# Where a partition's rows lie in DRAM: two runs of 785 and 367 rows in place of a block per transfer

## The chip, the cores and the metric

One core of a Trainium2 chip runs the kernel; the seven others are idle. The metric is the device time of one execution in microseconds (us), the median of several.

A ratio of two kernels is the mean time of one kernel's runs over that of the other's in the same rounds, with a 95% interval. It is thus not quite the quotient of the medians that are quoted beside it.

## The reference

```python
H = W = 384; C = 384; k = 1          # x: 1 x 384 x 384 x 384 in bf16, w1d: one number
g = jnp.einsum("bhwc->bc", x) / (H * W)
s = jax.nn.sigmoid(g * w1d[0])       # with k = 1 the convolution is one product
return x * s[:, None, None, :]
```

The gate s needs the mean over all 147,456 rows, so no row can be scaled before all were read. A row is 384 bf16 numbers, 768 B; each of 128 partitions gets 1152 rows, 884,736 B. The kernel keeps 367 rows per partition on the chip (296 of them folded, four into the space of three), and 785 are streamed through for the sum and read a second time for the product.

## The kernel before: the parts that matter

```python
def view(t, r0, n):                  # n rows a partition, one block of 128 n rows in DRAM
    return t[r0 * P : (r0 + n) * P, :].rearrange("(p r) c -> p r c", r=n)
...
def load(chunk, a, lo=0, hi=None):   # rows lo to hi of each partition's piece of the chunk
    r0, n = chunk
    ...  nc.sync.dma_start(out=arena[:, a : a + hi - lo, :], in_=view(xf, r0, n)[:, lo:hi, :])
...
def stream(n, a):
    load((streamed[0], n), a)        # a chunk of its own for each transfer
    ...  sum_rows(a, n)              # one matmul a row, into one accumulator
```

A chunk (r0, n) is a block of 128 n consecutive rows in DRAM, and partition p's piece of it is n rows starting at row p n of the block. The distance from one partition's piece to the next, the pitch, is therefore n x 768 B and depends on the transfer: 36,864 B for 48 rows. All large transfers are issued on one queue. While the stores and the second loads run, VectorE multiplies by s in place and restores the folded rows.

## Time and profile before

| quantity | value | from |
|---|---|---|
| time | 722.86 us (721.91 to 723.49) | 3 runs |
| span of the profiled run | 721.1 us | page |
| VectorE busy | 69% | busy times |
| TensorE busy | 30% | busy times |
| 16 DMA engines busy | 98.7% | table of queues |
| read and written | 190.41 and 113.25 MB | table of queues |

The table is read by asking which resource has no room left. It is the DMA engines; the lines of the page and of the stretches that carry this stand in the prediction. The chain of waits changes hands often (DMA 52%, VectorE 29% of it), but where VectorE is in the chain, DMA engines are still busy with other transfers, except at the turn from reading to writing.

### The profile page before, as it was taken

To read this page: it belongs to the slowest core of one execution; us is meant where nothing else is said; L and a number is where in the kernel's file an instruction comes from. 1 tells how busy PE (TensorE), PEld (TensorE's weight loads), DVE (VectorE), ACT (ScalarE), POOL (GpSimd) and SP (SyncE) were. 2 spreads that over 40 slices of the span, in tenths; PEclk is the share of its full clock that TensorE was granted. 3 is DMA by queue.
4 is the path that set the end of the run, shared out by engine and by line. 5 is a ranking of instruction groups with operands and counts; after the bars stand their busy time and mean duration, and the time that the engine had idled before them with its cause. 6 is when DMAs were issued, how large, how long until landed. Compare 5 with 4: busy or idle time off the path is not lost.

```text
span 721.1 us, 3241 instructions
## 1 busy us (share of the span) xinstructions
PE 212.8 (30%) x1202; PEld 118.5 (16%) x1202; DVE 496.3 (69%) x469; ACT 115.4 (16%) x92; POOL 0.2 (0%) x4
## 2 busy tenths in 40 slices
PE   4687788988877770000000000000000000000000
PEld 2344444554544340000000000000000000000000
DVE  4600003987999819999999998999979994355330
ACT  3600002765777610001100000000000000000000
POOL 0000000000000000000000000000000000000000
PEclk9899999999999995555555555555555555555555
DMA  9999999999999978999999999999999999999997
GB/s 377 438 432 426 429 433 428 435 431 425 430 422 429 426 329 333 413 426 427 436 429 439 423 431 436 433 439 426 419 432 433 440 437 427 426 435 437 438 428 321
DMA packets 19602, 303.87 MB, mean 421 GB/s; under 512 B 2178, under 2 KB 2178, under 8 KB 6402
## 3 DMA queue, kind: packets, MB, share of 16 engines
q1 hardware_dynamic: 19584, 303.67, 98.7%
q8 instruction: 9, 0.15, 0.1%
q14 instruction: 7, 0.06, 0.0%
q10 hardware_dynamic: 2, 0.00, 0.0%
HBM read 190.41 MB, written 113.25 MB: 421 GB/s over the span
## 4 chain that ended last, share of the span: by engine, by line
DMA 52%; DVE 29%; PE 6%; another core or an unknown queue 4%; ACT 3%; SPq 0%; issue 0%; DVEq 0%
DMA arena<-in_x_dram 37%; DVE arena L434 18%; DMA out_dram<-arena 15%; DVE arena L251 7%; PE bank L227 6%; DVE arena L257 4%; ACT arena L291 3%; SPq L221 0%; ACT s_bf L425 0%; PE bank L506 0%; DVE odd L501 0%; DVE odd_i L510 0%; DVE worst L496 0%; DVEq L112 0%
## 5 line engine op out<-in xcount | busy, mean ns | idle before, releaser
L434 DVE TENSOR_TENSOR arena<-arena,s_bf 128x1536 bf16<-128x1536 bf16 (+8 forms) x102 | 241.9, 2413 | 73.7 <-DMA arena<-in_x_dram 56.9
L251 DVE TENSOR_SCALAR arena<-arena 128x1536 uint16<-128x1536 uint16 (+2 forms) x247 | 145.9, 635 | 109.2 <-DMA arena<-in_x_dram 97.6
L227 PE MATMUL bank<-arena,ones 128*128 128x384 bf16 x1152 | 204.6, 339 | 55.0 <-DMA arena<-in_x_dram 54.9
L227 PEld LDWEIGHTS bank<-arena,ones 128*128 128x128 bf16 x1152 | 113.6, 101 | 145.7 <-DMA arena<-in_x_dram 60.4
L257 DVE TENSOR_TENSOR arena<-arena 128x1536 uint16<-128x1536 uint16 (+2 forms) x114 | 121.2, 1063 | 10.4 <-PE bank L227 8.3
L291 ACT ACTIVATE arena<-arena 128x3072 uint16<-128x3072 uint16 (+1 forms) x38 | 102.5, 2696 | 142.9 <-DVE arena L251 142.9
L361 ACT COPY arena<-bank 128x512 uint32<-128x512 uint32 (+1 forms) x7 | 4.0, 570 | 70.3 <-DMA out_dram<-arena 70.1
L242 PE MATMUL bank<-ones,zeros 128*128 128x384 bf16 x48 | 8.3, 326 | 0.0
L291 ACT ACTIVATION_READ_ACCUMULATOR arena<-arena 128x1 f32 x38 | 7.1, 187 | 0.0
L242 PEld LDWEIGHTS bank<-ones,zeros 128*128 128x128 bf16 x48 | 4.7, 98 | 3.1
L506 PE MATMUL bank<-odd,ones 128*128 128x1 bf16 x1 | 0.2, 187 | 15.8 <-DVE odd L501 15.8
L361 ACT COPY bank<-arena 128x512 uint32<-128x512 uint32 (+1 forms) x7 | 3.6, 565 | 0.0
L425 ACT ACTIVATE s_bf<-bank,w_sc 128x384 bf16<-128x384 f32 x1 | 0.6, 580 | 15.3 <-PE bank L227 15.3
L506 PEld LDWEIGHTS bank<-odd,ones 128*128 128x128 bf16 x1 | 0.1, 105 | 16.2 <-DVE odd L501 16.2
L721 ACT ACT_TABLE_LOAD x1 | 1.3, 1283 | 0.7 <-PEq L737 0.7
L321 DVE TENSOR_SCALAR w_sc<-bank 128x1 f32<-128x1 f32 x1 | 0.2, 160 | 1.1 <-PE bank L316 1.1
L311 DVE MEMSET ones<- 128x128 bf16 x1 | 0.2, 165 | 1.0 <-SPq L106 1.0
L316 PE MATMUL bank<-w_bf,ones 1*128 1x1 bf16 x1 | 0.2, 182 | 2.1 <-DMA w_bf<-in_w1d_dram 2.1
L316 PEld LDWEIGHTS bank<-w_bf,ones 1*128 1x128 bf16 x1 | 0.1, 100 | 2.1 <-DMA w_bf<-in_w1d_dram 2.1
L510 DVE CAST odd_i<-bank 128x1 int32<-128x1 f32 x1 | 0.2, 159 | 0.3 <-PE bank L506 0.3
L496 DVE TENSOR_REDUCE worst<-seen 128x1 f32<-128x38 f32 x1 | 0.2, 189 | 0.0
L501 DVE TENSOR_SCALAR odd<-worst 128x1 bf16<-128x1 f32 x1 | 0.2, 156 | 0.0
(5 smaller groups left out, 0.5 us busy)
## 6 DMA issues: line engine op xcount, KB each, us to landing
arena<-in_x_dram SPq DMA_DIRECT2D x17, 4608.0 KB, 34.7
out_dram<-arena SPq DMA_DIRECT2D x6, 4608.0 KB, 43.8
arena<-in_x_dram SPq DMA_DIRECT2D x19, 1248.0 KB, 11.7
arena<-in_x_dram SPq DMA_DIRECT2D x9, 2304.0 KB, 27.3
out_dram<-arena SPq DMA_DIRECT2D x8, 2304.0 KB, 28.7
arena<-in_x_dram SPq DMA_DIRECT2D x4, 4512.0 KB, 34.0
out_dram<-arena SPq DMA_DIRECT2D x3, 4512.0 KB, 26.7
out_dram<-arena SPq DMA_DIRECT2D x9, 1248.0 KB, 12.1
```

The costliest lines, as they stand in the source:

```text
L227: return nc.tensor.matmul(acc, lhsT=ones[:], rhs=arena[:, i, :], start=first, stop=last)
L242: lambda: nc.tensor.matmul(acc, lhsT=zeros[:], rhs=ones[:, None, :].to_broadcast([P, C // P, P]), start=False, stop=False),
L251: lambda: nc.vector.tensor_scalar(out=dst, in0=src, scalar1=s0, scalar2=s1, op0=op0, op1=op1),
L257: "DVE", lambda: nc.vector.tensor_tensor(out=dst, in0=a, in1=b, op=op), reads=reads, writes=writes
L291: lambda: nc.scalar.activation(out=y, in_=y, func=ACTF.Copy, accum_out=seen[:, 2 * k + i : 2 * k + i + 1]),
L311: fl.add("DVE", lambda: nc.vector.memset(ones[:], 1.0), writes=["ones"])
L316: lambda: nc.tensor.matmul(votes, lhsT=ones[0:1, :], rhs=w_bf[0:1, 0:1], start=True, stop=True),
L361: "ACT", lambda: nc.scalar.copy(dst.bitcast(u32), src.bitcast(u32)), reads=reads, writes=writes
L425: lambda: nc.scalar.activation(out=s_bf[:], in_=acc, func=ACTF.Sigmoid, scale=w_sc[:, 0:1]),
L434: lambda: nc.vector.tensor_tensor(out=v, in0=v, in1=s_bf[:, None, :].to_broadcast([P, n, C]), op=Op.mult),
L506: lambda: nc.tensor.matmul(votes, lhsT=ones[:], rhs=odd[:], start=True, stop=True),
L721: nc.scalar.preload_act_table(ACTF.Sigmoid)
```

## The change

The intent is to give each partition two fixed runs in DRAM, its 785 streamed rows together and its 367 kept rows together. Both counts are odd, so that neighbouring partitions lie an odd multiple of 256 B apart (768 B = 3 x 256 B) and large powers of two are avoided.

```diff
     N_STREAM = RPP - N_RAW - sum(4 * q for q in QS)
-    r = N_STREAM
+    N_KEPT = RPP - N_STREAM
+    assert N_STREAM % 2 and N_KEPT % 2
+    STREAMED, KEPT = (0, N_STREAM), (N_STREAM, N_KEPT)
+    r = 0
     ...
     def stream(n, a):
-        load((streamed[0], n), a)
+        load(STREAMED, a, streamed[0], streamed[0] + n)
     ...
     def group_load(g, lo, hi, a):
-        load(c_group[g], a, lo, hi)
+        load(KEPT, a, c_group[g] + lo, c_group[g] + hi)
     ...      # stores, raw rows and the second loads likewise; cut
```

More of the change, by code (lines that the diff above doesn't have):

```diff
@@ L203, with load @@
     N_STREAM = RPP - N_RAW - sum(4 * q for q in QS)
-    r = N_STREAM
+    N_KEPT = RPP - N_STREAM
+    assert N_STREAM % 2 and N_KEPT % 2
+    STREAMED, KEPT = (0, N_STREAM), (N_STREAM, N_KEPT)
+    r = 0
     c_group = []
     for q in QS:
-        c_group.append((r, 4 * q))
+        c_group.append(r)
         r += 4 * q
-    c_raw = (r, N_RAW)
-    assert r + N_RAW == RPP
+    c_raw = r
+    assert r + N_RAW == N_KEPT
     summed = [0]
-    def load(chunk, a, lo=0, hi=None):
+    def load(chunk, a, lo, hi):
         r0, n = chunk
-        hi = n if hi is None else hi
         fl.add(
@@ L415, in take_raw @@
     def take_raw(a, n):
-        load(c_raw, a, a - U, a - U + n)
+        load(KEPT, a, c_raw + a - U, c_raw + a - U + n)
         sum_rows(a, n)
@@ L522, in again @@
             turn = 0
-            for r0, n in c_group:
-                for lo in range(0, n, N_OVER):
-                    hi = min(n, lo + N_OVER)
+            for r0, q in zip(c_group, QS):
+                for lo in range(r0, r0 + 4 * q, N_OVER):
+                    hi = min(r0 + 4 * q, lo + N_OVER)
                     v = arena[:, Y : Y + hi - lo, :]
-                    pl.dma_start(out=v, in_=view(xf, r0, n)[:, lo:hi, :]).then_inc(moved, 16)
+                    pl.dma_start(out=v, in_=view(xf, *KEPT)[:, lo:hi, :]).then_inc(moved, 16)
                     pl.wait_ge(moved, 32 * turn + 16)
@@ L533, in again @@
                     pl.wait_ge(scaled, turn)
-                    pl.dma_start(out=view(of, r0, n)[:, lo:hi, :], in_=v).then_inc(moved, 16)
+                    pl.dma_start(out=view(of, *KEPT)[:, lo:hi, :], in_=v).then_inc(moved, 16)
                     pl.wait_ge(moved, 32 * turn)
@@ L592, in stored @@
         return f
-    landed.append((c_raw, Y, Y - U, 4, False))
-    landed.append((c_raw, Y + 4, Y - U + 4, 4, True))
-    landed.append((c_raw, T, T - U, 8, True))
-    landed.append((c_raw, U, 0, 8, True))
-    for e, n in ((0, 8), (8, 13), (21, 13), (34, 13)):
-        landed.append((c_raw, V + e, 8 + e, n, True))
+    for a, n, end in ((Y, 4, False), (Y + 4, 4, True), (T, 8, True), (U, 8, True), (V, 8, True)):
+        landed.append((KEPT, a, c_raw + a - U, n, end))
+    for a, n in SLOTS:
+        landed.append((KEPT, a, c_raw + a - U, n, True))
     HALVES = (T, U)
@@ L644, in start_pair @@
         f, t, _ = turns[-2]
-        turns[-2] = (f, t, lambda: send(c_group[g], a, 3 * lo, 3 * (lo + n), w_done, written))
+        turns[-2] = (f, t, lambda: send(KEPT, a, c_group[g] + 3 * lo, c_group[g] + 3 * (lo + n), w_done, written))
         f, t, _ = turns[-1]
-        turns[-1] = (f, t, lambda: send(c_group[g], at, 3 * QS[g] + lo, 3 * QS[g] + lo + n, u_done, written))
+        turns[-1] = (f, t, lambda: send(KEPT, at, c_group[g] + 3 * QS[g] + lo, c_group[g] + 3 * QS[g] + lo + n, u_done, written))
         return True
@@ L701 @@
             if n >= BIG or n == N_STREAM - todo or (ahead < LOW and n >= 8) or ahead < LAST:
-                chunk = (todo, n)
-                todo += n
-                load(chunk, a)
+                load(STREAMED, a, todo, todo + n)
                 for i in range(a, a + n):
                     idle[i] = False
-                parts = [(chunk, a + e, e, f - e, f == n) for e, f in split(n, PART)]
+                parts = [(STREAMED, a + e, todo + e, f - e, f == n) for e, f in split(n, PART)]
+                todo += n
                 moves.append([now + LAT, n * ROW + PER_LOAD, lambda parts=parts: landed.extend(parts)])
```

## The prediction

> **What bounds the kernel now.** I read the page from the top: the busy times, the forty slices, the table of queues; then the chain of waits in order of time, then the busy time by stretch, and last the packet records themselves.
>
> The slices come first, because they rank the engines at a glance.
>
> ```profile
> DVE  4600003987999819999999998999979994355330
> DMA  9999999999999978999999999999999999999997
> GB/s 377 438 432 426 429 433 428 435 431 425 430 422 429 426 329 333 413 426 427 436 429 439 423 431 436 433 439 426 419 432 433 440 437 427 426 435 437 438 428 321
> ```
>
> The DMA row is 9 in every slice but three (two in the middle, the last). VectorE is the only other candidate: it is high from slice 17 to 33 but falls to 3 to 5 near the end while the DMA row and the rate stay where they were. So VectorE is close behind but doesn't set the pace. The queue table says the same in one figure:
>
> ```profile
> q1 hardware_dynamic: 19584, 303.67, 98.7%
> HBM read 190.41 MB, written 113.25 MB: 421 GB/s over the span
> ```
>
> 98.7% of sixteen engines' 721.1 us is 711.7 us of work per engine. The tensor is 147,456 rows of 768 B, 113.25 MB, written once; it is read once, and the 785 streamed rows of each partition (785 x 128 x 768 B = 77.17 MB) a second time, which makes the 190.41 MB. No byte count changes in this change, so the rate and the gaps are all that can.
>
> The chain of waits, in order of time, shows where the gaps are:
>
> ```profile
> 3.78 41.18 DMA arena<-in_x_dram
> ...
> 254.81 12.12 DMA arena<-in_x_dram
> 266.98 2.79 PE bank L227 x16
> 270.40 14.84 DVE arena L434 x8
> ```
>
> Nothing moves before 3.78 us, and at 266.98 the last input has landed, the last sums and the sigmoid run, and the first store follows only after the first products. The stretches put sizes on it. The columns are the stretch, its length, the five engines' busy time with instruction counts, TensorE's clock, the DMA share and GB/s:
>
> ```profile
> 4.00:266.00 262.00, 208.74 (x1180) 116.48 (x1181) 138.19 (x190) 109.53 (x83) 0.00 (x0) 0.96 1.00 430
> 266.00:272.00 6.00, 3.69 (x22) 1.81 (x20) 1.60 (x2) 0.58 (x1) 0.00 (x0) 1.00 0.12 48
> 272.00:285.00 13.00, 0.00 (x0) 0.00 (x0) 13.00 (x7) 0.00 (x0) 0.00 (x0) 0.52 0.93 388
> 285.00:300.00 15.00, 0.19 (x1) 0.10 (x1) 14.62 (x17) 0.00 (x0) 0.00 (x0) 0.50 1.00 383
> 300.00:505.00 205.00, 0.00 (x0) 0.00 (x0) 197.97 (x170) 3.99 (x7) 0.00 (x0) 0.50 1.01 431
> 505.00:520.00 15.00, 0.00 (x0) 0.00 (x0) 14.90 (x15) 0.00 (x0) 0.00 (x0) 0.50 0.99 416
> 520.00:717.00 197.00, 0.00 (x0) 0.00 (x0) 115.64 (x70) 0.00 (x0) 0.00 (x0) 0.50 1.00 431
> ```
>
> About 5 us are idle at the turn (266 to 272 at a share of 0.12). Elsewhere the engines are busy all the time. Two stretches are odd: 285 to 300 and 505 to 520, where the share stays at 0.99 to 1.00 but the rate falls to 383 and 416 GB/s. Engines that are busy and move less are waiting for memory; that, and nothing else here, is what a layout in DRAM can touch.
>
> The packet records tell how much it is. Each transfer is 128 packets, one per partition, plus 16 writes of a semaphore: 136 large transfers, 17,408 packets. Of one size nearly all take the same time: 36,864 B take 1364 ns (the 10th, 50th and 90th percentile alike), 6,144 B take 234 ns. The slope is (1364 - 234) / 30,720 B = 0.0368 ns/B, 27.2 GB/s an engine and 435 for sixteen; the remainder is 8 ns a packet. So packets run at an engine's own rate, memory being ready in time. Adding up what each packet took above the median of its size, over all packets and divided by 16, gives 3.6 us in the whole run: 0.6 in the first transfer, 1.9 between 276 and 321 us of the span, 0.55 near 500 to 515, the rest in crumbs.
>
> Check of the sum: 303.67 MB / 435 GB/s = 698.1 us; 17,408 / 16 packets x 8 ns = 8.7; semaphore writes 1.2 (136 x 9 ns); excess 3.6. Together 711.6, against 711.7 in the table.
>
> **What the Trainium skill says.** "DMA: Bandwidth & Descriptors", section "Where 436 GB/s comes from", gives a ceiling of 435.2 GB/s from the SBUF ports; the slope above gives 435 in this trace, so they agree, and the section's warning that HBM would bind at about 358 GB/s for HBM transfers doesn't hold here (430 over 262 us). The page "HBM Reference", section "Specifications (TRN2)", gives 716 GB/s for a pair's memory and says a core alone is bounded by its DMA engines; that agrees, and leaves slack behind the engines. The table of "Latency and other measured facts" in the first page warns of a row pitch at large powers of two: 512 KiB ran at 207 GB/s a direction, 2 MiB at 164, 4 MiB at 103, and 4 MiB plus 4 KiB at 214, full rate. No run here has yet shown a bad pitch. "How a descriptor splits into AXI transactions" there says that a start off a 256 B boundary costs an extra transaction; 768 B rows always start on one, before and after.
>
> **The change part by part.** First, order: comparing the two built kernels, all instructions on all five engines and on the DMA queue come in the same sequence with the same shapes; only line numbers differ. So 136 transfers, 17,408 packets, 0 us from these, and the waits are the same waits.
>
> Second, what moves: addresses in DRAM alone. Before, a transfer of n rows took a block of 128 n rows, so neighbouring partitions' pieces lie n x 768 B apart: 36,864 B for 48 rows, 9,984 for 13, 49,152 for the groups of 64 kept rows, 54,528 for the 71 kept raw rows. After, they lie 785 x 768 = 602,880 B apart for streamed rows and 367 x 768 = 281,856 B for kept ones. Inside a packet it is one contiguous run of the same bytes both times, so packet sizes and the 8 ns stay: 0 us.
>
> Third, whether sixteen concurrent engines collide in memory. By the skill's "descriptor swizzle" (same page as above) neighbouring engines are four partitions apart. I work out that distance modulo 64 KiB as a rough proxy for spread over channels, whose real map I don't know. Before, 48 rows: 147,456, remainder 16,384, four distinct places for sixteen engines. The 64-row groups: 196,608, remainder 0, all on one place. Nevertheless 36,864 B packets have their 90th percentile at their median, so even a poor spread is not felt. After, streamed: 2,411,520, remainder 52,224 = 51 x 1024, with 51 odd; kept: 1,127,424, remainder 13,312 = 13 x 1024, 13 odd. Sixteen engines then fall on sixteen distinct kilobytes of the 64. That is what "odd" buys: 785 and 367 hold no factor of two, so the pitch is 256 B times an odd number. Both lie far from the bad powers of two. My estimate of the term: from -3.6 us (all excess gone) to a few us more; centre -0.5, since the two slow stretches sit at the turn from reading to writing and may have nothing to do with pitch.
>
> Fourth, reads and writes together after the turn: before, the store and the load of a moment lie in compact 4.7 MB blocks; after, each is spread over 128 places in 77 MB or 36 MB. A contiguous packet of 6 to 37 KB is long enough that I charge nothing for it.
>
> Sum: 722.86 + 0 + 0 - 0.5 + 0, rounded to 722.3 us.
>
> **Rivals.** (a) The excess disappears: spread over odd pitches takes the collisions away at 285 to 300 us. For: the rate there drops with the share at 1.00, and 9,984 B packets take 780 ns in place of 375. Against: the same pitches appear elsewhere at full rate. Time 719.3, not over 0.5% less. A larger gain is ruled out: 2% would be 14.5 us, four times all excess there is; the 5 us turn and the 3.8 us start aren't touched. (b) The spread hurts: 128 far places cost memory pages or another map than I assume, and packets run 2 to 4% longer throughout. 711 x 0.03 = 21 us, 744 us. For: packets touch far more distinct regions at a time, and the address map is unknown. Against: the skill's 512 KiB pitch at full rate, and 716 GB/s of memory behind 435. (c) Only the mixed stretch after the turn suffers, reads against writes: half of the packets slower by 1%, 355 x 0.01 = 3.6 us, 726.5. (d) Slower landings lengthen the turn or make VectorE wait; VectorE is busy 198 of 205 us from 300 to 505, so its slack is 7 us there and a hiccup could surface as a few us.
>
> **Range and chances.** (a) sets the low end, with the repeats of before spreading from 721.91 to 723.49: 718.5. (c) and (d) set the high end: 727.5. Faster by over 2% needs a term that no view has: 0.01. Slower by over 2% needs (b): 0.05. Within 2%: 0.94.
>
> **What would show it.** Right: queue table again at 303.67 MB and close to 98 to 99%; packets of 36,864 B again at 1364 ns and 6,144 B at 234; 4 to 266 us at about 430 GB/s; the turn at 0.12. For (a): 285 to 300 us above 400 GB/s and the summed excess under 2 us. For (b): DMA share at 1.00 with the rate under 420 in the read-only stretch too, medians off 1364. For (c): only stretches after 300 us drop. Wrong from the ground up would be a gap in the DMA share that isn't there now, as the waits themselves do not change.

## The result, and the profile after

After the change the kernel takes 722.75 us (722.28 to 723.06, 4 runs), beside 722.72 us before (721.91 to 723.49). The ratio is 1.0 with an interval from 0.9983 to 1.0017. The result is correct.

The page of the changed kernel, slices and queue, in the order in which the prediction has those of before:

```profile
DMA  9999999999999978999999999999999999999997
GB/s 382 425 447 424 425 429 433 435 434 420 433 424 427 428 326 334 418 427 431 433 429 442 416 433 436 436 443 418 433 431 436 429 440 435 420 436 438 434 432 305
...
q1 hardware_dynamic: 19584, 303.67, 98.6%
...
HBM read 190.41 MB, written 113.25 MB: 421 GB/s over the span
```

The DMA row is the same in all forty slices. Single slices of the rate wander by up to 16 GB/s in either direction. A packet is counted in the slice in which it starts, and one packet of 36,864 B on each of sixteen engines is, as an estimate, 33 GB/s of a slice of 18 us. The mean is 421 GB/s both times. The span is 721.1 us, as before to the tenth.

The same stretches of the changed kernel (columns as in the prediction: the engines' busy time and counts, TensorE's clock, DMA share, GB/s):

```profile
4.00:266.00 262.00, 211.74 (x1180) 117.77 (x1181) 138.10 (x190) 109.53 (x83) 0.00 (x0) 0.95 1.00 430
266.00:272.00 6.00, 3.63 (x22) 1.78 (x19) 1.66 (x2) 0.58 (x1) 0.00 (x0) 1.00 0.09 37
272.00:285.00 13.00, 0.00 (x0) 0.00 (x0) 13.00 (x7) 0.00 (x0) 0.00 (x0) 0.54 0.93 389
285.00:300.00 15.00, 0.19 (x1) 0.10 (x1) 14.62 (x18) 0.00 (x0) 0.00 (x0) 0.50 1.00 385
300.00:505.00 205.00, 0.00 (x0) 0.00 (x0) 196.85 (x170) 3.99 (x7) 0.00 (x0) 0.50 1.01 432
505.00:520.00 15.00, 0.00 (x0) 0.00 (x0) 14.90 (x15) 0.00 (x0) 0.00 (x0) 0.50 0.98 424
520.00:717.00 197.00, 0.00 (x0) 0.00 (x0) 116.50 (x70) 0.00 (x0) 0.00 (x0) 0.50 1.00 430
```

Against before, 430 stays 430 in the read-only stretch, 383 becomes 385, and the long stretches after the turn go from 431 to 432 and from 431 to 430. Two short ones differ more: the turn itself, 37 for 48 GB/s, worth 0.2 us, and 505 to 520 us, 424 for 416 GB/s, worth 15 us x 8 / 424 = 0.3 us the other way. The packet records agree: 36,864 B take 1364 ns and 6,144 B take 234 ns as before. "Excess" below means the time that a run's packets took above the median of their size in the same run, summed over all packets and divided by 16 engines. It is 3.0 us after against 3.6 before.

### The profile page after: what moved, and what is told of

Its sections match the earlier page's. It is cut to its first block, busy times and chain, and to the rows that moved or that the text cites. A ratio compares the mean times of both kernels' runs of the same rounds, so it can differ in the third digit from the quotient of the medians.

```text
span 721.1 us, 3241 instructions
## 1 busy us (share of the span) xinstructions
PE 215.7 (30%) x1202; PEld 119.8 (17%) x1202; DVE 496.0 (69%) x469; ACT 115.4 (16%) x92; POOL 0.2 (0%) x4
## 3 DMA queue, kind: packets, MB, share of 16 engines
q1 hardware_dynamic: 19584, 303.67, 98.6%
## 4 chain that ended last, share of the span: by engine, by line
DMA 53%; DVE 28%; PE 7%; another core or an unknown queue 4%; ACT 3%; SPq 0%; issue 0%; DVEq 0%
DMA arena<-in_x_dram 37%; DVE arena L437 18%; DMA out_dram<-arena 16%; PE bank L230 7%; DVE arena L254 6%; DVE arena L260 4%; ACT arena L294 3%; SPq L224 0%; ACT s_bf L428 0%; PE bank L509 0%; DVE odd L504 0%; DVE odd_i L513 0%; DVE worst L499 0%; DVEq L112 0%
## 5 line engine op out<-in xcount | busy, mean ns | idle before, releaser
L230 PE MATMUL bank<-arena,ones 128*128 128x384 bf16 x1152 | 207.6, 343 | 52.0 <-DMA arena<-in_x_dram 51.9
```

The costliest lines, as they stand in the source:

```text
L230: return nc.tensor.matmul(acc, lhsT=ones[:], rhs=arena[:, i, :], start=first, stop=last)
```

## The experiments

The theory: sixteen engines run at their own pace, memory behind them has slack, and a change of addresses that leaves packets and order alone is worth nothing. Rivals: oddness matters and the kernel before was merely lucky; two effects cancel; alignment matters; or nothing about a layout could ever matter. Each edit is made to the kernel after the change, unless said otherwise. "Wrong" means that the data are not the reference's, while transfers, sizes and waits are, except where a text says so. The diffs are shortened: what a helper function returns is written into the call, and lines are left out where "..." stands. Distances from engine to engine rest on the "descriptor swizzle" that the prediction cites; the packet records don't name the engine.

### One even run of 1152 rows

```diff
 def view(t, r0, n):
-    return t[r0 * P : (r0 + n) * P, :].rearrange("(p r) c -> p r c", r=n)
+    return t.rearrange("(p r) c -> p r c", r=RPP)[:, r0 : r0 + n, :]
```

> One run of 1152 rows per partition, an even pitch of 884,736 B (2^15 x 27). My theory (the sixteen engines set the pace, memory has slack, so addresses do not matter while packets stay the same): 722.7 us within 0.3%, 36,864 B packets at 1364 ns, summed packet excess 2 to 5 us. Rival 'odd matters' (an even pitch puts the engines on a few channels): over 735 us, with rates under 420 GB/s in the stretch from 4 to 266 us.

722.83 us, beside 722.88 before; ratio 1.0001 (0.9984 to 1.0017), correct. Excess 3.1 us, packets of 36,864 B at 1364 ns. A pitch with fifteen factors of two does as well as the odd ones, so the change's criterion isn't needed at this size of pitch.

### Only the kept rows in one run

```diff
-        load(STREAMED, a, streamed[0], streamed[0] + n)
+        load((streamed[0], n), a, 0, n)      # and the second loads and their stores likewise
```

> Only the kept rows lie in one run of 367; the streamed rows stay in a block per transfer as before. Theory: each half of the change is worth nothing, 722.7 us within 0.3%. Rival 'two effects cancel' (one half gains what the other loses): this half alone differs from before by over 0.5%, 3.6 us, either way.

722.66 us; ratio 1.0003 (0.9984 to 1.0022), correct. This half alone is worth nothing and both together are worth nothing, so the other half is too, within the intervals of 0.2%: no two effects cancel.

### Loads 128 B off

```diff
-        in_=view(xf, r0, n)[:, lo:hi, :]
+        at = r0 * P * C + (64 if r0 == 0 else -64)    # in elements of 2 B
+        in_=x1[at : at + n * P * C].rearrange("(p r c) -> p r c", r=n, c=C)[:, lo:hi, :]
```

> Every load starts 128 B off a 256 B boundary in DRAM (wrong result on purpose), everything else as after the change. If the skill's rule on transactions costs beats at the engine (my estimate: one more 256 B transaction, 8 beats of 32 B at 435 GB/s / 16, about 9 ns a packet; load packets are 190.4 of 303.7 MB, some 10,000 packets, 630 an engine): about 6 us more, 728 to 730, and packets of 36,864 B that load take about 1373 ns against 1364 for those that store. If the alignment of the source is hidden behind the write side: 722.7 us and no second packet time.

722.71 us; ratio 0.9996 (0.998 to 1.0013), wrong. No packet time moved (36,864 B: 1364 ns at the 10th and the 90th percentile). Loads don't pay for this shift, and my estimate of 6 us fell. It was also too high by its own source. By the table in the Trainium skill, "DMA: Bandwidth & Descriptors", section "How a descriptor splits into AXI transactions", a start 128 B off makes the first transaction 8 beats but shortens the last to 4, so a packet whose size is a multiple of 256 B takes 4 beats more, not 8. That is an estimate of 4.7 ns a packet and 3.0 us for the 640 load packets of an engine, which the interval (at most 0.9 us) excludes as well.

### Loads at a pitch of exactly 512 KiB

```diff
+        ...
+        first = lo % (PITCH // C - 48)                # PITCH = 262,144 elements
+        v = x1[at : at + P * PITCH].rearrange("(p e) -> p e", e=PITCH)
+        in_=v[:, first * C : (first + hi - lo) * C].rearrange("p (r c) -> p r c", c=C)
```

> All loads at a pitch of exactly 512 KiB per partition[...] (wrong result on purpose); stores as after. If memory's slack covers even a large power of two at one reading core: 722.7 us within 0.5%. If such a pitch folds the engines on few channels: over 760 us, packets of loads over 1500 ns and the stretch from 4 to 266 us much longer, which shows that layout can matter and that both kernels lie on the flat part.

724.07 us beside 722.88; ratio 1.0016 (0.9999 to 1.0032), wrong. Excess 4.3 us against 3.0; the read-only stretch stays at 430 GB/s, and from 300 to 505 us, where loads lie between stores, the rate is 429 for 432. So even this power of two costs the loads 0.2%, at the edge of what the interval can tell from nothing.

### Every row a run of its own

```diff
 def view(t, r0, n):
-    return t[r0 * P : (r0 + n) * P, :].rearrange("(p r) c -> p r c", r=n)
+    return t.rearrange("(r p) c -> p r c", p=P)[:, r0 : r0 + n, :]
```

> Partition p holds the rows p, p + 128, p + 256 and so on, so that every row of 768 B is a run of its own in DRAM, for loads and stores; result correct. Theory (time is packets at 8 ns plus bytes at 27.2 GB/s an engine, wherever they lie): 303.67 MB / 768 B / 16 = 24,700 packets an engine x (28.2 + 8) ns = 895 us, plus the 9 to 10 us of start, turn and end: about 905 us, with packets of 768 B near 36 ns. Rival 'only bytes count': about 723 us. Rival 'scattered short runs cost memory time as well': over 1000 us and packets well over 36 ns.

830.48 us beside 722.4; ratio 1.1498 (1.1475 to 1.1521), correct. The time is none of the three that were named; only the packet's recorded 36 ns came out as the theory had it. The lines of its page (rate in forty slices, packets, queue):

```profile
GB/s 320 373 372 372 373 372 372 372 372 372 371 372 371 371 321 316 372 372 372 373 373 373 373 373 373 373 373 372 373 373 372 373 373 372 373 373 373 373 373 310
DMA packets 397586, 303.87 MB, mean 367 GB/s; under 512 B 2178, under 2 KB 397570, under 8 KB 397570
...
q1 hardware_dynamic: 397568, 303.67, 107.7%
```

A share of 107.7% can't be a share of time: the records of consecutive packets overlap. A packet of 768 B is recorded with 36 ns, as predicted, but at 373 GB/s one passes every 768 / (373 / 16) = 32.9 ns. At 27.2 GB/s its bytes take 28.2 ns, so a packet costs 4.7 ns on top of its bytes, and the remaining 3 ns of its record lie under its neighbour. The records of the kernel before overlap too: up to 21 are open at once, on sixteen engines. The rate is constant to 1 GB/s over most slices, so no scatter in memory shows.

### All partitions of a load read the same rows

```diff
-        in_=view(xf, r0, n)[:, lo:hi, :]
+        in_=xf[r0 + lo : r0 + hi, :][None, :, :].to_broadcast([P, hi - lo, C])
```

> Every partition of a load reads the same rows in DRAM, so that all sixteen engines ask for the same addresses at about the same time (wrong result on purpose). It is the extreme of a collision. Theory of memory slack, which the pitch of 512 KiB did not exhaust: not known whether it holds here; if it does, 722.7 us within 0.5% and 1364 ns packets. If the engines then share few channels: reads slow down, over 760 us and medians of loads off 1364 ns. For the stretch from 285 to 300 us: if its lost rate comes from reads and writes opening different pages in memory, it rises over 400 GB/s, else it stays at 370 to 390.

726.25 us beside 722.4; ratio 1.0058 (1.0042 to 1.0075), wrong. That is at the edge of the theory's band (726.3 us; by the ratio 0.08% over it), far under the rival's. Medians are unchanged, excess 6.5 us. The stretch from 285 to 300 us fell to 368 GB/s rather than rise over 400, so that idea of its cause found no support.

### Stores 128 B off

```diff
-        out=view(of, r0, n)[:, lo:hi, :]
+        out=o1[at : at + n * P * C].rearrange("(p r c) -> p r c", r=n, c=C)[:, lo:hi, :]   # at as above
```

> Every store starts 128 B off a 256 B boundary in DRAM (wrong result on purpose), loads as after the change. Theory after the shifted loads cost nothing: stores cost nothing either, 722.7 us within 0.3%. Rival (the write side pays for a partial transaction at both ends of a packet): 17,408 packets less some 10,000 loads, 430 an engine x 9 to 18 ns, 4 to 8 us more, with stores of 36,864 B at 1373 to 1382 ns.

724.3 us beside 722.4; ratio 1.0032 (1.0016 to 1.0049), wrong. Sizes that only stores have show it: the median packet of 10,752 B goes from 404 to 408 ns, of 12,288 B from 460 to 465, of 21,504 B from 799 to 804. There are 56 stores, 56 x 128 / 16 = 448 packets an engine, so some 4 to 5 ns each make 2 us, which is what was measured. The time alone would not decide: it lies within 0.3% of 722.7 us, as the theory had it, and short of the rival's 4 to 8 us. The packet times do, and they fit the 4 beats (4.7 ns by estimate) worked out above for loads. Stores pay for the shift, loads don't.

### Four short runs for one

```diff
-        in_=view(xf, r0, n)[:, lo:hi, :]
+        block = x1[(r0 + lo) * P * C : (r0 + hi) * P * C]
+        in_=block.rearrange("(h p e) -> p h e", h=4, p=P)      # stores likewise
+        ...                                                   # and the on-chip side in four pieces
```

> Each partition's run of a transfer is cut into four equal runs that lie apart in DRAM, so 69,632 packets in place of 17,408, 3,264 more per engine; bytes and order as after (wrong result on purpose, since loads and stores cut differently). Which cost a packet has is what it tells: with the 8 ns of the prediction, 26 us more, 749 us; with what the interleaved rows gave (768 B every 32.9 ns at 373 GB/s, 4.7 ns over 28.2), 15 us more, 738 us; with none, 722.7.

738.26 us beside 722.86; ratio 1.0213 (1.0196 to 1.023), wrong. The rise of 15.4 us over 3,264 more packets an engine is 4.7 ns each. Two layouts with very different packets give one figure (the whole time of the interleaved rows gives 4.6: 108.1 us over 23,624 more packets an engine), and here it was forecast: 738 us.

### Stores at a pitch of exactly 2 MiB

```diff
+    PITCH = 2 * 524288                                         # elements
+    far = nc.dram_tensor("far", (P * PITCH,), bf16, kind="Internal").ap()
+    ...                       # the first streamed rows and the last kept ones still go to the output
-        out=view(of, r0, n)[:, lo:hi, :]
+        v = far.rearrange("(p e) -> p e", e=PITCH)
+        out=v[:, (r0 + lo) * C : (r0 + hi) * C].rearrange("p (r c) -> p r c", c=C)
```

> Nearly all stores go to another region of DRAM at a pitch of exactly 2 MiB per partition, 8 MiB from engine to engine (the result is wrong on purpose, most of the output isn't written); loads as after. Control that a layout can hurt at all: by the skill's table 2 MiB ran at 164 against 207 GB/s for copies within DRAM; if that is a limit on one direction of 164 to 207 GB/s, stores of 113 MB take 550 to 690 us in place of 260, and the time is over 850 us; if it is a ratio of 0.79, stores take about 70 us more, 790 us. If engines still set the pace with one core's store stream: 722.7 us within 0.5%.

787.64 us beside 722.86; ratio 1.0882 (1.0853 to 1.091), wrong. This is the control that was missing: a layout can hurt. Of the estimates named, the ratio of 0.79 (790 us) came close. Its stretches, of which the first, without stores, is untouched:

```profile
4.00:266.00 262.00, 212.39 (x1181) 118.01 (x1182) 138.10 (x190) 109.63 (x83) 0.00 (x0) 0.95 1.00 430
...
272.00:285.00 13.00, 0.00 (x0) 0.00 (x0) 13.00 (x8) 0.00 (x0) 0.00 (x0) 0.55 1.05 244
285.00:300.00 15.00, 0.18 (x1) 0.10 (x1) 8.79 (x13) 0.00 (x0) 0.00 (x0) 0.50 0.99 187
300.00:505.00 205.00, 0.00 (x0) 0.00 (x0) 157.10 (x134) 4.00 (x7) 0.00 (x0) 0.50 1.01 354
```

The share stays near 1 while the rate falls, by about half from 272 to 300 us and to 354 GB/s after that, with packets and their sizes unchanged: engines wait inside packets. The median packet of the one store of 12,288 B packets takes 570 ns in place of 460. The excess is 61.9 us by the run's own medians, which rose for such stores; by the medians of the kernel before it is 67.0, 64.0 more than in the changed kernel, and 64.8 us were lost. Packets of 36,864 B, most of them loads, keep 1364 ns at the 10th, 50th and 90th percentile even here, so one size alone can hide a loss. This is the signature that the changed kernel does not have.

### The kernel before, once more

> The kernel before once more, for the noise of the profile: the excess of 0.55 us near 505 to 520 us and the rate of 416 GB/s there were in its first profile and in none of the others. If it is noise: 505 to 520 above 420 GB/s, total excess about 3 us, and the stretch from 285 to 300 at 383 again. If it belongs to the block layout: both come back.

723.15 us in a single run (its state is therefore unknown; it is used for the profile only), correct. Two stretches of its trace:

```profile
285.00:300.00 15.00, 0.19 (x1) 0.10 (x1) 14.62 (x17) 0.00 (x0) 0.00 (x0) 0.50 1.01 379
...
505.00:520.00 15.00, 0.00 (x0) 0.00 (x0) 14.90 (x15) 0.00 (x0) 0.00 (x0) 0.50 0.99 426
```

The 416 GB/s of 505 to 520 us did not come back, so the 0.3 us that the changed kernel seemed to gain there is noise. The dip from 285 to 300 us did, with a total excess of 3.5 us.

### Stores at 2 MiB less 4 KiB

The edit is that of the 2 MiB stores with PITCH less 2048 elements.

> As the stores at a pitch of 2 MiB, to the same other region of DRAM, but at 2 MiB less 4 KiB (wrong result on purpose). If the power of two is what cost 65 us, and 4 KiB off it is enough as the skill's table has it for 4 MiB: 722.9 us within 1%. If it is the other region, or the distance as such: about 788 us again.

726.48 us beside 722.34; ratio 1.0051 (1.0035 to 1.0068), wrong. It is the power of two, not the other region or the size of the pitch as such, that cost the 65 us; some 4 us remain (excess 8.3 us).

### Stores at 2 MiB less 256 B

The same with PITCH less 128 elements, so that the pitch is 256 B x 8191, an odd number.

> The same at 2 MiB less 256 B, which is 256 B times 8191, an odd number: the change's own criterion (an odd multiple of 256 B) right beside a power of two. If oddness is what protects, 722.9 us within 1%. If it is the distance from the power of two: the sixteen engines then write 8 MiB less 1 KiB apart, and the time stays well above, 745 to 790 us.

756.74 us beside 722.34; ratio 1.0466 (1.0447 to 1.0485), wrong. Its stretches:

```profile
285.00:300.00 15.00, 0.19 (x1) 0.10 (x1) 11.96 (x16) 0.00 (x0) 0.00 (x0) 0.50 0.99 287
300.00:505.00 205.00, 0.00 (x0) 0.00 (x0) 169.48 (x144) 4.00 (x7) 0.00 (x0) 0.50 1.01 378
```

The profiled run, at 762.41 us the slowest of four, has an excess of 38.0 us. An odd multiple of 256 B is no protection next to a large power of two; keeping 4 KiB away from it was, but for 4 us. Where between 256 B and 4 KiB the loss ends was not tried.

One more kernel, with stores at 512 KiB folded back into the output, was refused before it ran, because stores then overlapped in DRAM without order (my account; neither this attempt nor the next left a run). Whether stores mind 512 KiB as little as loads do is open. So is 2 MiB for loads: reading a region that nothing had written was refused as well.

## Why the prediction was right

**What bounds the kernel.** Right. The engines are busy, packets go at 27.2 GB/s plus a fixed cost, and no more than a few microseconds of memory waiting existed to be won. Excess is 3.0 to 3.6 us in the layouts that cost nothing (e1 to e3, before and after) and rises one for one with the time where a layout does cost (64.0 us more against 64.8 us lost, the packets measured by the medians of the kernel before). One sentence of it was too wide: engines that are busy and move less need not be waiting for memory. With rows of 768 B (e5) the rate is 372 GB/s at a full share because there are more packets.

**Order and packets unchanged.** Right: 19,584 packets on the queue, 303.67 MB, the same stretches.

**The addresses: -0.5 us.** Measured 0.0 with an interval of about 1.2 us either way, so the term's size is met, but its grounds were poor. I counted distinct places modulo 64 KiB and wrote that this "is what 'odd' buys". It bought nothing: an even pitch of 2^15 x 27 B does the same (e1), 512 KiB puts all engines on one such place and costs loads 0.2% (e4), and an odd pitch beside 2 MiB costs 4.7% (e12). The proxy ranks the two pitches beside 2 MiB the wrong way round: less 256 B gives sixteen distinct places and costs 4.7%, less 4 KiB gives four and costs 0.5%. Nor was it enough that packets of 36,864 B have their 90th percentile at their median, since they have it at 2 MiB too (e9); the small excess over all sizes was the better ground. The step came out right because both layouts are far from any large power of two in the sense that the stores at 2 MiB (e9, e11) show; oddness had no part in it, so the reason that the step gave was not why it held.

**Rival (a), the excess disappears.** Refuted: the dip from 285 to 300 us is 383, 379, 385, 384 and 389 GB/s in before, before again, after, e1 and e2. It comes with the turn from loads to stores; pitch didn't make it. The prediction's "9,984 B packets take 780 ns" holds for few of them: 47 of the 450 in this stretch take over 5% more than 375 ns. And 1.35 of the stretch's 1.46 us of excess lie between 285.6 and 289 us, some 3 us after the first load behind the turn is issued (282.98 us). What makes these packets slow was not found, only that the same rows for all partitions don't cure it. The other slow stretch, 505 to 520 us, does not sit at the turn, as the prediction has it; it was noise (e10).

**Rivals (b), (c), (d).** Refuted for this change: outside the turn no stretch lost more than 1 GB/s, and the time is the same. Rival (b) was set aside with the skill's "512 KiB pitch at full rate"; the table has 207 GB/s there and 214 for full rate, and in e4 it cost loads 0.2%. That (b) exists as a mechanism is shown by e9; its signature, a share near 1 at a low rate, was named rightly, but it appeared only where stores ran.

**The sum.** Here a term was mis-sized. The prediction took 8 ns a packet from recorded times and closed the sum at 711.6 us against 711.7. Both sides were sums of records, and records overlap by some 3 ns, so the agreement proved less than it seemed. In time a packet costs 4.7 ns (e5, e8): 17,408 / 16 x 4.7 = 5.1 us, not 8.7. By the same sum (698.1 + 5.1 + 1.2 + 3.6 = 708.0 of 721.1 us) the time that an engine has no work is, as an estimate, 13 us rather than 9.4. Counting the open records at each moment agrees: they fall short of sixteen by 13.7 us of the span. Nothing of this moved the predicted time, since packets did not change.

**256 B boundaries: 0 us.** Right, as both layouts keep them. What leaving them would cost was tested: nothing for loads (e3), 2 us for stores (e7).

No experiment points to a version that beats both kernels: each one is at best the same.

## What to carry to other kernels

Before moving data about in DRAM, look at whether packets of each size already take one time, and add up what they take above it. Here that excess was 3.6 us, and no layout with the same packets gained anything; fewer or longer packets, fewer bytes or smaller gaps are what is left to try. If a layout is changed anyway, keep each packet's run long (4.7 ns a packet) and the pitch some KiB away from a large power of two; an odd row count by itself guarantees nothing. A share of busy engines near 1 at a falling rate, with packets of the same sizes, is how a bad pitch looked; shorter packets look alike (e5). All of this was measured with one core running; with neighbours that use the same memory it is open.

## What the Trainium skill lacked or had wrong

- "DMA: Bandwidth & Descriptors", "How a descriptor splits into AXI transactions": an extra transaction for a start off 256 B did not show on loads from DRAM (722.71 us at 128 B off, ratio 0.9996); stores paid 4 to 5 ns a packet (404 to 408 ns at 10,752 B). By the section's beats 128 B off is 4.7 ns a packet, an estimate at 27.2 GB/s an engine, so the stores fit it and the loads don't; the section doesn't separate the two.
- The same page, "Latency and other measured facts", row pitch: it has copies within DRAM only. For stores from on-chip memory beside loads, 2 MiB cost 8.8%, 2 MiB less 4 KiB 0.5%, 2 MiB less 256 B 4.7%; for loads, 512 KiB cost 0.2%, within noise. Its advice to stay a few KiB off holds here, and so does its warning that a few hundred bytes aren't enough, though 256 B took away about half of the loss (34.4 us for 64.8).
- The same page, "Why small descriptors are slow (HBM only)": the cost of a packet in DRAM transfers is 4.7 ns in time, from 768 B packets at 373 GB/s and from 15.4 us for 3,264 more packets an engine. It puts it at about 3 cycles, by my estimate 3.5 ns at the 850 MHz of "Where 436 GB/s comes from"; the measured figure is higher. The section also names 32 B of metadata for each descriptor, by estimate 1.2 ns at 27.2 GB/s, which would make up the difference; no run here shows it apart.
- No page says that packet records overlap in a profile ("DMA: Bandwidth & Descriptors", section "Two DMAs through the same engine are not ordered", says only that the descriptors of a queue are pipelined): 107.7% of sixteen engines' span, 36 ns recorded for a packet that passes every 32.9 ns.
